# A two-dimensional DFT and a gated layer on one core: the second DFT stage as 64x64 products on four quadrants of the array

## The chip, the cores and the metric

The kernel runs on one core of one Trainium2 chip. The metric is device time in microseconds (us) of one execution, as the median over repeated executions; lower is better. TensorE (PE) does matrix products and writes PSUM; VectorE (DVE), ScalarE (ACT) and GpSimd (POOL) work on SBUF, the first two on PSUM too; SyncE (SP) issues most of the transfers. Each engine runs its own instructions in order and waits on semaphores of the others. In the profile "PE" rows are matmuls and "PEld" rows are the weight loads that go with them.

## The reference

```python
# x: (8, 3008, 256) f32, w_in: (256, 2048), w_out: (2048, 256)
X = np.fft.fft(x, axis=1)
X = np.fft.fft(X, axis=2)
y = X.real.reshape(8 * 3008, 256)
h = y @ w_in
out = (h * np.cos(h)) @ w_out          # (24064, 256)
```

## The kernel before

**How the sums are split.** The DFT over 256 features is folded into the weights once, at the start: `w_in` becomes `WC` (for the real part of the sequence DFT) and `WS` (for its imaginary part). What is left for each of the 8 batches is the DFT over the 3008 positions. 3008 is 47 times 64, and it is done in two stages. The first stage (`first_half` for batch 0, `first_half_later` for the others) takes sums over 47 rows and writes `z` to DRAM, which is read back with its parts in another order (`store_z`, `load_z`). The second stage (`second_half`) takes sums over 64 values with the table `BJ`. It gives, for each of six groups `g` of four columns `jj`, two tiles of 128 features by 256 positions: an "even" part (e = 0, multiplied by `WC`) and an "odd" part (e = 1, multiplied by `WS`), both kept in `pq`. Group 0 uses 225 of the 256 positions (`_width`).

**The table before.** In `z` as loaded, the rows of the even and the odd part are interleaved over the 128 partitions. One matmul for each `jj` contracts all 128 partitions against a 128x128 block of `BJ`, whose columns 0 to 63 give the even part and 64 to 127 the odd part. Half of each block is zero: a row that belongs to the even part has zeros in the odd columns, and the other way round. The four products of a group fill one PSUM bank `pb`, and one ScalarE copy (L540) sorts it into `pq`.

**The main loop.** The gated layer runs in 8 x 6 x 8 = 384 steps: batch, group, and eight pairs of 128-wide slices of the 2048 hidden values (`fp`). A step's work is spread over several turns of the loop at L1068, because it passes through the engines: at turn t the current step `cur` gets its products with `WC` and `WS` (`mm1`, L719) into a PSUM bank `H`; ScalarE doubles it (L730), VectorE subtracts (L735), ScalarE rounds (L750) and takes the sine (L760), VectorE does the rest (L754, L764, L775, L785), and three turns later (`LAG`) `mm2` (L810) multiplies by combinations of `w_out` into accumulators `M`. A turn of 256 positions has two `mm1` products with `WC`, four products of `mm2`, two of `mm1` with `WS`, and three of `mm2`, in this order. Every f32 product appears in the profile as two weight loads and two matmuls.

**PSUM.** Eight banks: `M` four, `H` three, and a single one of tag `fft`, shared in turn by the first stage (`pz`) and the second (`pb`). `H` of the next step is set to 0.25 plus a rank-one term by ScalarE (`seed`, L689) before `mm1` adds to it.

**Where the DFT of the next batch goes.** While batch b-1 goes through the layer, `transform(b)` places the DFT of batch b at turns counted from the start of batch b-1 (offset 0 to 47; 48 and up is the next batch's first turns). First-stage products run at offsets 12, 20, 28 and 36 as a "session" between `mm1(cur, 0)` and `mm2(done, 0)`: 64x64 products on the four quadrants of the array, with two outputs, one in the `fft` bank and one in the `H` bank that the next step will use. ScalarE copies the `H` part out at once (`take_half`), before `seed` overwrites that bank, and the `fft` part at the end of the turn (`take_first`). VectorE folds the input for these sessions (`fold_pair`, L364) at offsets 8 to 11, 16 to 19, and so on, and writes the results of a finished group out by transposes (L912) at offsets 6, 7, 14, 15 and so on. `z` is loaded at offset 38. The six groups of the second stage run at the end of turns 42, 44, 46, 49, 52 and 55 (49, 52 and 55 are turns 1, 4 and 7 of the next batch). Batch 0 has its own places: group 0 in the opening, the others at turns 5, 10, 14, 18 and 22 (`opening`). After each group two small transfers on SP (L549, L550) spread row 0 of the odd part over 128 partitions as `nb`, which `seed` reads.

Of the kernel before, what the change touches and what calls it, by code (L numbers as in the profile page):

```python
# [11 lines left out]
FP = mybir.dt.float32  # L12
# [9 lines left out]
NJ = 24  # L22
# [23 lines left out]
def _consts():  # L46

    s2 = np.arange(N2)  # L50
    j = np.arange(NJ)
    th = 2.0 * np.pi * np.outer(s2, j) / N2
    thm = 2.0 * np.pi * np.outer(46 - s2, j) / N2
    thh = 2.0 * np.pi * np.outer(s2 + 0.5, j) / N2
    z = np.zeros((N2, NJ))
    pad = np.zeros((2 * N2, 16))

    def stack(a, b, c, d):
        m = np.block([[a, b], [c, d]]).reshape(2 * N2, 2, NJ)
        near, far = m[:, :, 0:JA], m[:, :, JA:]  # L60
        return near.reshape(2 * N2, 2 * JA), far.reshape(2 * N2, 2 * (NJ - JA)), pad

    LE = stack(np.cos(th), -np.sin(th), np.cos(thm), -np.sin(thm))
    LO = stack(np.sin(th), np.cos(th), -np.sin(thm), -np.cos(thm))
    LE0 = stack(np.cos(th), z, z, np.cos(thh))
    LO0 = stack(np.sin(th), z, z, np.sin(thh))
    LM, LO, LM0, LO0 = (np.concatenate(m, axis=1) for m in (LE, LO, LE0, LO0))
    LE, LE0 = (np.concatenate(m[::-1], axis=1) for m in (LE, LE0))
    L = np.concatenate([LE, LO, LE0, LO0, -LO, LM, LM0], axis=1)
    rows = np.zeros((128, NL))  # L70
    for side in range(2):
# [12 lines left out]
    i = np.arange(NI)  # L84
    B = np.zeros((128, NJ, 128))
    for jj in range(NJ):
        phi = 2.0 * np.pi * np.outer(i, 47 * k2 + jj) / SEQ
        blk = np.concatenate([np.cos(phi), np.sin(phi)], axis=0)
        blk[0] = 1.0
        blk[NI] = np.where(k2 % 2 == 0, 1.0, -1.0)  # L90
        blk = blk.reshape(2, 2, 16, 64)
        for half in range(2):
            for r in range(2):
                for e in range(2):
                    p = 64 * half + 2 * e + r
                    B[p : p + 61 : 4, jj, 64 * e : 64 * e + 64] = blk[r, half]

    c = np.arange(ND)
    d = np.arange(128)
    ang = 2.0 * np.pi * np.outer(c, d) / ND  # L100
    CS = np.concatenate([np.cos(ang), -np.sin(ang)], axis=1) / TWO_PI
    CS[:, 128] = np.where(c % 2 == 0, 1.0, -1.0) / TWO_PI
    CS = CS[0:128].reshape(128, 2, 64, 2).transpose(0, 1, 3, 2).reshape(128, 256)
    return (
        L.astype(np.float32),
        B.reshape(128, NJ * 128).astype(np.float32),
        CS.astype(np.float32),
    )

# [27 lines left out]
def kernel(  # L137
# [92 lines left out]
    BJ = cpool.tile([128, NJ * 128], FP, tag="BJ", name="BJ")  # L230
    w2 = cpool.tile([128, 16 * ND], FP, tag="w2", name="w2")

    def load_w(q):
# [204 lines left out]
    zss = {}  # L438
    pairs = {}

    def first_half(b, c):

        LE, LO, LE0, LO0, NLO, LM, LM0 = (L[0:XR, 64 * q : 64 * q + 64] for q in range(7))
# [28 lines left out]
                    fv = home(c, e).rearrange("r (i d) -> r i d", d=128)[0:XR]  # L472
                    product(e, i0, i1, e, w[e], fv[:, i0:i1, e:128])
        if c < 4:
            if c // 2 not in pairs:
                pairs[c // 2] = spool.tile([128, 1024], FP, tag="zs", bufs=2, name="zs")
            zs = pairs[c // 2][:, 512 * (c % 2) : 512 * (c % 2) + 512]
        else:
            zs = spool.tile([128, 512], FP, tag="pq", bufs=8, name="zs")
        take_z(zs, pz)  # L480
        zss[b, c] = zs

# [27 lines left out]
            if queue is nc.gpsimd and far:  # L510
                beside(sent, near_z)

    def load_z(b, far, rows=slice(0, 128)):
        if b not in z2s:
            z2s[b] = spool.tile([128, NJ * 128], FP, tag="z2", bufs=1, name="z2")
        cols = slice(128 * JA, None) if far else slice(0, 128 * JA)
        return nc.sync.dma_start(out=z2s[b][rows, cols], in_=zds[b, far][rows])

    ready = {}

    def second_half(b, g):

        T = _width(g)
        z2 = z2s[b]
        pb = psum("pb")
        pq = spool.tile([128, 512], FP, tag="pq", bufs=8, name="pq")
        pv = pq.rearrange("d (e q k) -> d e q k", e=2, k=64)
        bv = pb.rearrange("d (q e k) -> d e q k", q=4, e=2)
        for q in range(4):
            jj = 4 * g + q  # L530
            at = 128 * ((q + 3) % 4 if g == 0 else q)
            nc.tensor.matmul(  # L532
                pb[:, at : at + 128],
                lhsT=z2[:, jj * 128 : jj * 128 + 128],
                rhs=BJ[:, jj * 128 : jj * 128 + 128],
                start=True,
                stop=True,
            )
        if b or g:
            nc.scalar.copy(out=pv, in_=bv)  # L540
        else:
            nc.scalar.copy(out=pv[:, 1], in_=bv[:, 1])
            nc.vector.tensor_copy(out=pv[:, 0], in_=bv[:, 0])
        nb = spool.tile([128, 256], FP, tag="nb", bufs=6, name="nb")
        ready[b, g] = (pq, nb)
        if b == 0 and g < 2:
            return
        nd = dpool.tile([1, 256], FP, tag="nd", bufs=4, name="nd")
        nc.sync.dma_start(out=nd[:, 0:T], in_=pq[0:1, 256 : 256 + T])  # L549
        nc.sync.dma_start(out=nb[:, 0:T], in_=nd[0:1, 0:T].to_broadcast([128, T]))  # L550


    def spread_norm(g, tag):
        T = _width(g)
        pq, nb = ready[0, g]
        pn = psum("pn", tag)
        nc.tensor.matmul(pn[:, 0:T], lhsT=first, rhs=pq[:, 256 : 256 + T], start=True, stop=True)
        return nb[:, 0:T], pn[:, 0:T]

    def keep_norm(out, in_):  # L560
# [7 lines left out]
    def transform(b):  # L568
# [13 lines left out]
                between.setdefault(t0 + o + e + 1, []).append((fold_pair, c, e))  # L582
        for k in range(NCH // 2):
            o = 12 + 8 * k
            sessions[t0 + o] = b, k
            at(o, take_first, b, k)
            at(o + 1, store_z, b, k, 0)
            at(o + 1, store_z, b, k, 1)
# [3 lines left out]
            between.setdefault(t0 + f, []).append((fold_edge, e))  # L592
        at(38, load_z, b, 0)
        at(38, load_z, b, 1)
        for g, o in enumerate((42, 44, 46, 49, 52, 55)):
            at(o, second_half, b, g)

    def split_sum(n):
        nc.vector.tensor_tensor(out=plus[n], in0=wr[n][0], in1=wr[n][1], op=ALU.add)
# [28 lines left out]

    def keep_row(e, n, pw, _):
        if n > 1:  # L630
            nrow[n] = spool.tile([128, 512], FP, tag="pq", bufs=8, name="nrow")
        nc.vector.tensor_copy(out=nrow[n][0:1, :], in_=pw[0:1, :])

    def fold(e, n, tag="M", row=False):
# [66 lines left out]
    def seed_first(s):  # L701
        T, c0 = s.T, 256 * (s.fp % 2)
        s.pq, s.nb = ready[s.b, s.grp]
        for u in range(2):
            nc.tensor.matmul(  # L705
                s.H[:, u * T : u * T + T],
                lhsT=nrow[s.fp // 2][:, c0 + 128 * u : c0 + 128 * u + 128],
                rhs=s.pq[:, 256 : 256 + T],
                start=False,
                stop=True,  # L710
                skip_group_check=True,
            )

    def mm1(s, e):
        T = s.T
        W = WS if e else WC
        for u in range(2):
# [1 line left out]
            nc.tensor.matmul(  # L719
                s.H[:, u * T : u * T + T],  # L720
                lhsT=W[:, 128 * f : 128 * f + 128],
                rhs=s.pq[:, 256 * e : 256 * e + T],
                start=False,
                stop=True,
                skip_group_check=True,
# [235 lines left out]
    for n in range(3):  # L961
# [2 lines left out]
        fill = fold_weights(0, n)  # L964
        keep_fold(*fill)
        if n == 0:
            beside(load_bj(0, 512), fill[3])
        if n < 2:
            split_sum(n + 2)
            split_rest(n + 2)  # L970
        keep_row(*row)
    for s in steps[0:3]:
        fill_first(s)
    load_z(0, 0, slice(0, 112))
    near_z = load_z(0, 0, slice(112, 128))
    for c in order[:4]:
        store_z(0, c, 1)
    for row in range(2):
# [4 lines left out]
    for k, c in enumerate(order[4:]):  # L983
        store_z(0, c, 1)
        if k:
            take_columns((1, 2, 0)[k - 1])
    load_bj(512, 1024)
    second_half(0, 0)
    late = fold_weights(1, 3, units=(0,))
    combine_w2(0, 2, nc.vector)  # L990

    opening = {
        5: ((second_half, 0, 1),),
        6: ((lambda: keep_norm(*spread_norm(1, "fft")),),),
        8: ((load_bj, 1536, NJ * 128),),
        10: ((second_half, 0, 2), (load_ident,)),
        14: ((second_half, 0, 3),),
        18: ((second_half, 0, 4),),
        22: ((second_half, 0, 5),),
    }  # L1000
# [58 lines left out]
    for call in todo.pop(LAG - 1, ()):  # L1059
        call[0](*call[1:])  # L1060
    load_v()
    load_bj(1024, 1536)

    def step(t, last=None):
        s = steps[t] if 0 <= t < n else None
# [2 lines left out]
    for t in range(LAG, n + LAG + 1):  # L1068
# [91 lines left out]
```

## Time and profile before

| | |
|---|---|
| median of 3 runs | 1914.87 us (1914.58 to 1915.2) |
| the profiled execution | 1914.27 us, span 1912.5 us |
| granted TensorE clock, mean | 0.999 of full speed |
| PE matmuls | 9334 records, busy 1899.5 us |
| DVE | 3340 instructions, busy 1782.8 us |
| ACT | 2681 instructions, busy 1490.9 us |
| POOL | busy 414.9 us |
| second-stage matmuls (pb, L532) | 384 records, median 275 ns |
| second-stage copies (pq, L540) | 47, median 585 ns |
| first-stage matmuls of batches 1 to 7 (L396, 64x64 quadrants) | 482 to 642 ns for 384 to 512 columns |

Durations of matmuls overlap, since the next starts while the last one drains; what a matmul costs is read from the distance of two starts. The busy time of an engine is the union of its instructions. The idle time of an engine, and what ended it, is shown beside a group of instructions.

### The profile page before, as it was taken

The numbers are of one execution on the slowest core, as the hardware profiler recorded it, in microseconds if no ns is written. First come the engines' busy times: TensorE is split into PE (matmuls) and PEld (weight loads), VectorE is DVE, ScalarE is ACT, GpSimd is POOL, SyncE is SP. The second block draws the span as 40 slices with busy tenths as digits, with TensorE's granted clock in tenths as the row PEclk, the third lists the DMA queues.
The fourth block names the chain that finished last, engine by engine and source line by source line (L and its number), as shares of the span: only waits on it lengthen the run. The fifth ranks groups of instructions, "written<-read, shape, count | busy, mean of one in ns | idle before, by whom it ended". The sixth has DMA issues, their size and how long they took to land.

```text
span 1912.5 us, 29405 instructions
## 1 busy us (share of the span) xinstructions
PE 1899.5 (99%) x9334; PEld 1688.3 (88%) x9334; DVE 1782.8 (93%) x3340; ACT 1490.9 (78%) x2681; POOL 414.9 (22%) x493
## 2 busy tenths in 40 slices
PE   8999999999999999999999999999999999999998
PEld 5888899888998889988898888988889888898887
DVE  7999989999899998999999999999999999999998
ACT  5777777778777877788777877788777887787775
POOL 5422112221122211222112221122211222111111
PEclk9999999999999999999999999999999999999999
DMA  7321211113111221111311113101231011210001
GB/s 239 81 52 48 79 45 26 27 47 81 38 28 29 49 80 32 31 29 45 88 28 28 28 45 90 31 22 28 54 87 30 19 23 27 59 24 10 13 21 23
DMA packets 157386, 89.15 MB, mean 47 GB/s; under 512 B 106374, under 2 KB 151903, under 8 KB 154891
## 3 DMA queue, kind: packets, MB, share of 16 engines
q1 hardware_dynamic: 153823, 83.48, 17.1%
q0 software_dynamic: 1376, 1.84, 0.4%
q10 hardware_dynamic: 2032, 1.95, 0.3%
q8 instruction: 74, 1.21, 0.3%
q14 instruction: 81, 0.66, 0.1%
HBM read 49.94 MB, written 37.28 MB: 46 GB/s over the span
## 4 chain that ended last, share of the span: by engine, by line
PE 97%; DVE 1%; DMA 0%; issue 0%; ACT 0%; ACTq 0%; SPq 0%; DVEq 0%
PE M L810 59%; PE H L719 34%; PE pb L532 2%; PE pz L396 1%; DMA xp<-in_x_dram 0%; PE pz L453 0%; DVE r L764 0%; PE pw L610 0%; DVE r L754 0%; DVE S L775 0%; PE H L396 0%; DMA z<-zd 0%; DVE h L735 0%; DVE xp L214 0%; PE H L705 0%
## 5 line engine op out<-in xcount | busy, mean ns | idle before, releaser
L810 PE MATMUL M<-S,VX 128*128 128x256 f32 (+1 forms) x2304 | 612.7, 375 | 0.0
L810 PEld LDWEIGHTS M<-S,VX 128*128 128x128 f32 x2304 | 438.6, 190 | 49.1
L750 ACT ACTIVATE r<-H 128x512 f32<-128x512 f32 (+1 forms) x384 | 226.1, 589 | 283.5 <-DVE h L735 280.7
L760 ACT ACTIVATE r<-r 128x1024 f32<-128x1024 f32 (+1 forms) x384 | 395.6, 1030 | 24.6 <-DVE r L754 17.2
L810 PE MATMUL M<-r,w 128*128 128x256 f32 (+1 forms) x1536 | 391.1, 377 | 0.0
L719 PE MATMUL H<-pq,WS 128*128 128x256 f32 (+1 forms) x1536 | 388.1, 375 | 0.9 <-ACT ew L730 0.9
L719 PE MATMUL H<-pq,WC 128*128 128x256 f32 (+1 forms) x1536 | 387.8, 375 | 0.0
L689 ACT ACTIVATE H<-nb,wn 128x256 f32<-128x256 f32 (+1 forms) x762 | 361.2, 474 | 13.3
L735 DVE TENSOR_TENSOR h<-ew,H 128x512 f32<-128x512 f32 (+1 forms) x384 | 259.0, 674 | 94.4 <-PE H L719 86.0
L719 PEld LDWEIGHTS H<-pq,WS 128*128 128x128 f32 x1536 | 292.1, 190 | 34.8 <-ACT ew L730 2.4
L810 PEld LDWEIGHTS M<-r,w 128*128 128x128 f32 x1536 | 298.4, 196 | 26.1
L719 PEld LDWEIGHTS H<-pq,WC 128*128 128x128 f32 x1536 | 288.6, 190 | 29.2
L754 DVE SCALAR_TENSOR_TENSOR r<-r,H 128x512 f32<-128x512 f32 (+1 forms) x384 | 258.7, 674 | 18.0
L730 ACT ACTIVATE ew<-H 128x512 f32<-128x512 f32 (+1 forms) x384 | 225.6, 587 | 51.7 <-PE H L719 45.5
L862 POOL TENSOR_TENSOR cb<-cb,mr 128x256 f32<-128x256 f32 (+3 forms) x190 | 159.3, 849 | 484.8 <-DVE S L785 343.0
L775 DVE TENSOR_TENSOR S<-r 128x512 f32<-128x512 f32 (+1 forms) x384 | 259.7, 676 | 0.1
L754 DVE SCALAR_TENSOR_TENSOR r<-r,h 128x512 f32<-128x512 f32 (+1 forms) x384 | 259.2, 675 | 0.0
L764 DVE SCALAR_TENSOR_TENSOR r<-h,r 128x512 f32<-128x512 f32 (+1 forms) x384 | 258.5, 673 | 0.0
L764 DVE SCALAR_TENSOR_TENSOR r<-H,r 128x512 f32<-128x512 f32 (+1 forms) x384 | 256.3, 667 | 0.4
L750 ACT ACTIVATE r<-h 128x512 f32<-128x512 f32 (+1 forms) x384 | 235.6, 613 | 0.0
L339 POOL TENSOR_TENSOR xs<-xp 113x512 f32<-113x512 f32 x112 | 143.0, 1276 | 403.2 <-DVE S L785 309.9
L810 PE MATMUL M<-S,w 128*128 128x256 f32 (+1 forms) x768 | 226.9, 377 | 1.2 <-DVE S L785 1.1
(106 smaller groups left out, 1531.6 us busy)
## 6 DMA issues: line engine op xcount, KB each, us to landing
out_dram<-ob SPq DMA_DIRECT2D x726, 32.0 KB
xp<-in_x_dram SPq DMA_DIRECT2D x256, 56.0 KB
z<-zd SPq DMA_DIRECT2D x8, 1280.0 KB
zd<-zs SPq DMA_DIRECT2D x120, 80.0 KB
nb<-nd SPq DMA_DIRECT2D x39, 128.0 KB
xp<-in_x_dram SPq DMA_DIRECT2D x52, 48.0 KB
xp<-in_x_dram SPq DMA_DIRECT2D x42, 49.0 KB
w<-in_moe_w_out_dram SPq DMA_DIRECT2D x4, 512.0 KB
```

What stands on the lines that cost most here:

```text
L339: return nc.gpsimd.tensor_tensor(out=rows_of(c, e)[0:XL], in0=xv[:, 0], in1=xv[:, 1], op=ALU.subtract if e else ALU.add,)
L689: nc.scalar.activation(out=s.H[:, u * T : u * T + T], in_=s.nb[:, 0:T], func=AF.Copy, bias=0.25, scale=wn[:, f : f + 1],)
L719: nc.tensor.matmul(s.H[:, u * T : u * T + T], lhsT=W[:, 128 * f : 128 * f + 128], rhs=s.pq[:, 256 * e : 256 * e + T], start=False, stop=Tr ...
L730: nc.scalar.mul(out=s.ew[:, 0 : 2 * s.T], in_=s.H[:, 0 : 2 * s.T], mul=2.0)
L735: return nc.vector.tensor_tensor(out=s.h[:, 0 : 2 * T].rearrange("p (u t) -> p u t", u=2)[:, :, ::-1], in0=s.ew[:, 0 : 2 * T].rearrange("p ...
L750: nc.scalar.activation(out=r, in_=h, func=AF.Copy, bias=BIG, scale=1.0)
L754: nc.vector.scalar_tensor_tensor(out=r, in0=r, scalar=-BIG, in1=h, op0=ALU.add, op1=ALU.subtract)
L760: nc.scalar.activation(out=r, in_=r, func=AF.Sin, bias=0.0, scale=SIN_SCALE)
L764: nc.vector.scalar_tensor_tensor(out=r, in0=h, scalar=-0.25, in1=r, op0=ALU.add, op1=ALU.mult)
L775: return nc.vector.tensor_tensor(out=sv[:, 0:2], in0=gv[:, 2:3].to_broadcast([128, 2, T]), in1=gv[:, 0:4:3], op=ALU.subtract,)
L810: nc.tensor.matmul(acc[key][m // 2][:, 256 * (m % 2) : 256 * (m % 2) + T], lhsT=w, rhs=a, start=first, stop=s.fp == 7, skip_group_check=True,)
L862: return nc.gpsimd.tensor_tensor(out=o, in0=a, in1=b, op=ALU.subtract if less else ALU.add)
```

## The change

The second stage is cut into 64x64 products. The even rows of `z` go to partitions 0 to 63 and the odd rows to 64 to 127 (a transposed read in `load_z`), so `BJ` has one 64x64 block for each part and no zeros, and half its size. Each `jj` takes four products: features 0 to 63 or 64 to 127 (u), times even or odd part (e). The two parts go to different PSUM banks. Two groups are done in one call (`second_pair`), as a session like those of the first stage, with the even part in the `fft` bank and the odd part in the next step's `H` bank. The three calls of a batch stand at offsets 44, 53 and 61. In batch 0, groups 0 and 1 stay single calls, and the others are pairs at turns 13 and 21. `pq`, `nb` and the two small transfers cover two groups at a time.

```diff
-    B = np.zeros((128, NJ, 128))
+    B = np.zeros((128, NJ, 64))
...
-                    p = 64 * half + 2 * e + r
-                    B[p : p + 61 : 4, jj, 64 * e : 64 * e + 64] = blk[r, half]
+                    p = 64 * e + 32 * r + 16 * half
+                    B[p : p + 16, jj] = blk[r, half]
...
-    def load_z(b, far, rows=slice(0, 128)):
+    def load_z(b, far):
...
-        return nc.sync.dma_start(out=z2s[b][rows, cols], in_=zds[b, far][rows])
+        return nc.sync.dma_start(
+            out=z2s[b][:, cols], in_=zds[b, far].rearrange("(x q) c -> q x c", q=4)
+        )
...
-    def second_half(b, g):
-
-        T = _width(g)
+    def second_products(b, groups, homes, clear=(True, True)):
         z2 = z2s[b]
-        pb = psum("pb")
...
-        for q in range(4):
-            jj = 4 * g + q
-            at = 128 * ((q + 3) % 4 if g == 0 else q)
-            nc.tensor.matmul(
-                pb[:, at : at + 128],
-                lhsT=z2[:, jj * 128 : jj * 128 + 128],
-                rhs=BJ[:, jj * 128 : jj * 128 + 128],
-                start=True,
-                stop=True,
-            )
+        for n, g in enumerate(groups):
+            for q in range(4):
+                jj = 4 * g + q
+                at = 256 * n + 64 * ((q + 3) % 4 if g == 0 else q)
+                for u in range(2):
+                    for e in range(2):
+                        first = n == q == 0 and clear[e]
+                        nc.tensor.matmul(
+                            homes[e][64 * u : 64 * u + 64, at : at + 64],
+                            lhsT=z2[64 * e : 64 * e + 64, 128 * jj + 64 * u : 128 * jj + 64 * u + 64],
+                            rhs=BJ[64 * e : 64 * e + 64, 64 * jj : 64 * jj + 64],
+                            start=first,
+                            stop=True,
+                            skip_group_check=not first,
+                        )
...
+    def second_half(g):
+        pb = psum("pb")
+        if g == 0:
+            homes, clear = (pb[:, 0:256], psum("pb", "M")[:, 0:256]), (True, True)
+        else:
+            homes, clear = (pb[:, 0:256], acc[0, 0][3][:, 256:512]), (True, False)
+        second_products(0, (g,), homes, clear)
+        halves = hold(0, g)
+        nc.scalar.copy(out=halves[1], in_=homes[1])
+        (nc.scalar.copy if g else nc.vector.tensor_copy)(out=halves[0], in_=homes[0])
+
+    def second_pair(b, k, after):
+        pb = psum("pb")
+        after.H = psum("H", "H")
+        second_products(b, (2 * k, 2 * k + 1), (pb, after.H))
+        for g in (2 * k, 2 * k + 1):
+            hold(b, g)
+        pqs[b, k] = pb
+
+    def take_pair(b, k, e, src):
+        pq, nb = held[b, k]
+        nc.scalar.copy(out=pq[:, 512 * e : 512 * e + 512], in_=src)
+        if e:
+            nd = dpool.tile([1, 512], FP, tag="nd", bufs=4, name="nd")
+            nc.sync.dma_start(out=nd, in_=pq[0:1, 512:1024])
+            nc.sync.dma_start(out=nb, in_=nd[0:1].to_broadcast([128, 512]))
+
+    def take_plus(b, k):
+        take_pair(b, k, 0, pqs[b, k])
...
-            sessions[t0 + o] = b, k
+            sessions[t0 + o] = first_half_later, take_half, b, k
...
-        for g, o in enumerate((42, 44, 46, 49, 52, 55)):
-            at(o, second_half, b, g)
+        later_pair(t0 + 44, b, 0)
+        later_pair(t0 + 53, b, 1)
+        later_pair(t0 + 61, b, 2)
+
+    def later_pair(t, b, k):
+        sessions[t] = second_pair, take_pair, b, k
+        todo.setdefault(t, []).append((take_plus, b, k))
...
-    load_z(0, 0, slice(0, 112))
-    near_z = load_z(0, 0, slice(112, 128))
+    near_z = load_z(0, 0)
...
-    load_bj(512, 1024)
-    second_half(0, 0)
+    load_bj(256, 512)
+    second_half(0)
...
-        5: ((second_half, 0, 1),),
+        5: ((second_half, 1),),
...
-        8: ((load_bj, 1536, NJ * 128),),
-        10: ((second_half, 0, 2), (load_ident,)),
-        14: ((second_half, 0, 3),),
-        18: ((second_half, 0, 4),),
-        22: ((second_half, 0, 5),),
+        10: ((load_ident,),),
...
+    later_pair(13, 0, 1)
+    later_pair(21, 0, 2)
...
-            first_half_later(*session, step(t + 1))
+            session[0](*session[2:], step(t + 1))
...
-            take_half(*session, 1, step(t + 1).H)
+            session[1](*session[2:], 1, step(t + 1).H)
```

More of the change, by code (lines that the diff above doesn't have):

```diff
@@ L105, in _consts @@
         L.astype(np.float32),
-        B.reshape(128, NJ * 128).astype(np.float32),
+        B.reshape(128, NJ * 64).astype(np.float32),
         CS.astype(np.float32),
@@ L229 @@
     plus = [w[:, 1024:1536] for w in staged[0:2]] + [more[:, 0:512], more[:, 512:1024]]
-    BJ = cpool.tile([128, NJ * 128], FP, tag="BJ", name="BJ")
+    BJ = cpool.tile([128, NJ * 64], FP, tag="BJ", name="BJ")
     w2 = cpool.tile([128, 16 * ND], FP, tag="w2", name="w2")
@@ L439, with half_tile @@
     pairs = {}
+    def half_tile(name, n, tag="pq", bufs=4):
+        at = name, n // 2
+        if at not in pairs:
+            pairs[at] = spool.tile([128, 1024], FP, tag=tag, bufs=bufs, name=name)
+        return pairs[at][:, 512 * (n % 2) : 512 * (n % 2) + 512]
     def first_half(b, c):
@@ L474, in first_half @@
         if c < 4:
-            if c // 2 not in pairs:
-                pairs[c // 2] = spool.tile([128, 1024], FP, tag="zs", bufs=2, name="zs")
-            zs = pairs[c // 2][:, 512 * (c % 2) : 512 * (c % 2) + 512]
+            zs = half_tile("zs", c, "zs", 2)
         else:
-            zs = spool.tile([128, 512], FP, tag="pq", bufs=8, name="zs")
+            zs = half_tile("zs", c)
         take_z(zs, pz)
@@ L516, in load_z @@
         cols = slice(128 * JA, None) if far else slice(0, 128 * JA)
-        return nc.sync.dma_start(out=z2s[b][rows, cols], in_=zds[b, far][rows])
+        return nc.sync.dma_start(
+            out=z2s[b][:, cols], in_=zds[b, far].rearrange("(x q) c -> q x c", q=4)
+        )
     ready = {}
-    def second_half(b, g):
-        T = _width(g)
+    def second_products(b, groups, homes, clear=(True, True)):
         z2 = z2s[b]
-        pb = psum("pb")
-        pq = spool.tile([128, 512], FP, tag="pq", bufs=8, name="pq")
-        pv = pq.rearrange("d (e q k) -> d e q k", e=2, k=64)
-        bv = pb.rearrange("d (q e k) -> d e q k", q=4, e=2)
-        for q in range(4):
-            jj = 4 * g + q
-            at = 128 * ((q + 3) % 4 if g == 0 else q)
-            nc.tensor.matmul(
-                pb[:, at : at + 128],
-                lhsT=z2[:, jj * 128 : jj * 128 + 128],
-                rhs=BJ[:, jj * 128 : jj * 128 + 128],
-                start=True,
-                stop=True,
-            )
-        if b or g:
-            nc.scalar.copy(out=pv, in_=bv)
-        else:
[L542 to L550, printed above, removed]
@@ new lines, in hold @@
+    def hold(b, g):
+        at = b, g // 2
+        if at not in held:
+            held[at] = (
+                spool.tile([128, 1024], FP, tag="pq", bufs=4, name="pq"),
+                spool.tile([128, 512], FP, tag="nb", bufs=3, name="nb"),
+            )
+        pq, nb = held[at]
+        c0 = 256 * (g % 2)
+        halves = pq[:, c0 : c0 + 256], pq[:, 512 + c0 : 768 + c0]
+        ready[b, g] = halves, nb[:, c0 : c0 + 256]
+        return halves
+    held = {}
+    def second_half(g):
+        pb = psum("pb")
+        if g == 0:
+            homes, clear = (pb[:, 0:256], psum("pb", "M")[:, 0:256]), (True, True)
+        else:
+            homes, clear = (pb[:, 0:256], acc[0, 0][3][:, 256:512]), (True, False)
[3 more added lines that the diff above has]
+        (nc.scalar.copy if g else nc.vector.tensor_copy)(out=halves[0], in_=homes[0])
@@ new lines, in second_pair @@
+    def second_pair(b, k, after):
[5 more added lines that the diff above has]
+        pqs[b, k] = pb
+    pqs = {}
+    def take_pair(b, k, e, src):
[5 more added lines that the diff above has]
+            nc.sync.dma_start(out=nb, in_=nd[0:1].to_broadcast([128, 512]))
@@ L556, in spread_norm @@
         pn = psum("pn", tag)
-        nc.tensor.matmul(pn[:, 0:T], lhsT=first, rhs=pq[:, 256 : 256 + T], start=True, stop=True)
+        nc.tensor.matmul(pn[:, 0:T], lhsT=first, rhs=pq[1][:, 0:T], start=True, stop=True)
         return nb[:, 0:T], pn[:, 0:T]
@@ L630, in keep_row @@
         if n > 1:
-            nrow[n] = spool.tile([128, 512], FP, tag="pq", bufs=8, name="nrow")
+            nrow[n] = half_tile("nrow", n)
         nc.vector.tensor_copy(out=nrow[n][0:1, :], in_=pw[0:1, :])
@@ L707, in seed_first @@
                 lhsT=nrow[s.fp // 2][:, c0 + 128 * u : c0 + 128 * u + 128],
-                rhs=s.pq[:, 256 : 256 + T],
+                rhs=s.pq[1][:, 0:T],
                 start=False,
@@ L721, in mm1 @@
                 lhsT=W[:, 128 * f : 128 * f + 128],
-                rhs=s.pq[:, 256 * e : 256 * e + T],
+                rhs=s.pq[e][:, 0:T],
                 start=False,
@@ L966 @@
         if n == 0:
-            beside(load_bj(0, 512), fill[3])
+            beside(load_bj(0, 256), fill[3])
         if n < 2:
@@ L1061 @@
     load_v()
-    load_bj(1024, 1536)
+    load_bj(512, NJ * 64)
     def step(t, last=None):
```

## The prediction

> **What bounds the kernel now.** I read the page's busy shares first, then the chain that ended last.
>
> ```profile
> PE 1899.5 (99%) x9334; PEld 1688.3 (88%) x9334; DVE 1782.8 (93%) x3340; ACT 1490.9 (78%) x2681; POOL 414.9 (22%) x493
> ...
> PE 97%; DVE 1%; DMA 0%; issue 0%; ACT 0%; ACTq 0%; SPq 0%; DVEq 0%
> PE M L810 59%; PE H L719 34%; PE pb L532 2%; PE pz L396 1%; DMA xp<-in_x_dram 0%; PE pz L453 0%; DVE r L764 0%; PE pw L610 0%; DVE r L754 0%; DVE S L775 0%; PE H L396 0%; DMA z<-zd 0%; DVE h L735 0%; DVE xp L214 0%; PE H L705 0%
> ```
>
> PE sets the time from end to end, and the second stage (`pb`, L532) is 2% of it, on that chain. So time taken from it is gained, unless PE then waits. VectorE at 93% is the engine it could wait for.
>
> Next the timeline of PE around one group (columns: start, length, engine, line):
>
> ```profile
> 237.03 1.05 PE L532 MATMUL pb<-BJ,z 128*128 128x128 f32 x8
> 237.92 1.03 PE L719 MATMUL H<-pq,WC 128*128 128x256 f32 x4
> ```
>
> Eight records from 237.03 to 237.92: a group costs 0.89 us, 0.111 for each record. In the second row four records of 256 columns take 0.86 to the next start, 0.215 each, so 0.84 ns a column; 128 columns are 0.107, and each short record pays 0.004 more.
>
> Third, a first-stage session, the only place where all four quadrants work:
>
> ```profile
> 163.66 0.60 PE L719 MATMUL H<-pq,WC 128*128 128x256 f32 x2
> 164.19 0.64 PE L396 MATMUL pz<-xf,V 49*64 49x512 f32 x1
> 164.19 0.64 PE L396 MATMUL H<-xf,V 49*64 49x512 f32 x1
> 164.20 0.64 PE L396 MATMUL pz<-xf,V 49*64 49x512 f32 x1
> 164.21 0.64 PE L396 MATMUL H<-xf,V 49*64 49x512 f32 x1
> 164.66 0.59 PE L396 MATMUL pz<-xf,V 49*64 49x512 f32 x1
> ...
> 165.14 0.20 PE L396 MATMUL pz<-xs,V 49*64 49x4 f32 x1
> ...
> 165.27 1.14 PE L810 MATMUL M<-r,w 128*128 128x256 f32 x4
> ```
>
> Four products start within 0.02 us of each other and run together; their second records follow 0.47 later (427 ns of columns and 0.05 for the first weight load, which nothing hides: 0.64 against 0.59). Entering costs 0.09: the last 256-column record starts at 163.88, is through at 164.09, and the quadrants start at 164.19. Leaving costs 0.12 from 165.14 to 165.27, and 0.11 for the open weight load of the next product (1.14 against 1.03).
>
> **The second stage in quadrants.** A pair of groups is 32 products, 64 records, 16 for each quadrant. A record of 64 columns is 0.054 of columns and, like the short ones above, 0.004 more: 0.058. The weight loads give the same: two single-column records of one quadrant late in a session have their loads 0.06 apart, so a 64-wide load just hides behind 64 columns. Bounds: 0.054, and 0.070 (a 512-column record in a quadrant is followed after 0.443, 16 ns over its columns). I take 0.058, since the record it comes from is the nearest in length. A pair is then 0.09 + 0.05 + 16 x 0.058 + 0.10 + 0.11 = 1.28 us; leaving is taken as 0.10 (0.09 after the fold of the weights at 27.84, 0.12 here). Two groups cost 1.78 now, so 0.50 is saved, for 23 pairs (3 in each of batches 1 to 7, 2 in batch 0): **-11.5 us**. Groups 0 and 1 of batch 0 stay single, 0.82 for 0.89; group 0 lies in the opening where PE waits, and I count 0.3 for it.
>
> **What else moves, at nothing.** ScalarE copies as much as before (two of 0.585 for two groups), but the odd part's copy now comes before the next `seed`; sessions have the same copy there, and the `seed` behind it still ends 2.4 us before its `mm1` (322.58 to 324.95). The SP queue gets 23 row transfers and 23 spreads for 46 each, and the odd part of a pair is there three turns (over 12 us) before `seed` needs it, two turns for the pair at turn 13; in the old timeline a spread is issued 1.1 to 3.6 us after its row. `BJ` is half the bytes. The near `z` load of batch 0 becomes one transfer of 128 rows that waits for the last store, where 112 rows went 0.43 us ahead; PE waited 1.4 us for it. This can cost 0 to 0.5, once; I take 0. The copy from half of an accumulator bank (group 1) can hold `mm2` by at most 0.6, once, in turns where PE waits for VectorE anyway.
>
> **First wait: the `fft` bank.** The last pair of each batch stands at offset 13, one turn after the session at 12, whose even half must leave the bank first:
>
> ```profile
> 324.95 1.03 PE L719 MATMUL H<-pq,WC 128*128 128x256 f32 x4
> ```
> ```profile
> 325.66 0.58 ACT L384 COPY zs<-pz 128x512 f32<-128x512 f32 x1
> ```
>
> PE is through with `mm1` at 325.81 and, with 0.09 to enter, ready for the pair at 325.90. The copy ends at 326.24, and the closest that a matmul follows its input's writer in this trace is 0.05. PE waits 0.39, and behind it in its queue `mm2` and all of the turn. This holds at turns 13, 61, 109, 157, 205, 253, 301 and at 21 (after the session at 20); 349 has no session before it. **+3.1 us** (0 if the copy comes sooner, 4 if the handover takes 0.15).
>
> **Second wait: VectorE at offsets 8 to 11.** There VectorE folds inputs and writes transposes, and a turn of group 0 is short for PE. PE's last product of a turn reads `S`, whose last part VectorE has just written. The two timelines from turn 151 on (offset 7 in batch 3):
>
> ```profile
> 768.15 1.05 PE L532 MATMUL pb<-BJ,z 128*128 128x128 f32 x8
> ...
> 773.06 0.55 PE L810 MATMUL M<-S,w 128*128 128x225 f32 x2
> ...
> 781.84 0.55 PE L810 MATMUL M<-S,w 128*128 128x225 f32 x2
> ...
> 786.54 0.66 PE L810 MATMUL M<-S,w 128*128 128x256 f32 x2
> ```
> ```profile
> 771.85 0.38 DVE L785 TENSOR_TENSOR S<-r,S 128x225 f32<-128x225 f32 x1
> ...
> 781.23 0.38 DVE L785 TENSOR_TENSOR S<-r,S 128x225 f32<-128x225 f32 x1
> ...
> 785.95 0.42 DVE L785 TENSOR_TENSOR S<-r,S 128x256 f32<-128x256 f32 x1
> ```
>
> The margins are 0.83, 0.23 and 0.17 us. From 763 on VectorE has no break but short ones behind its own work (ScalarE's rounding), and 0.11 that it waits for PE before L735 at 772.57. The group at 768.15, which gives it 0.89, goes away; the pair at offset 53 stands too early to help, as VectorE has caught up by 54. So PE comes 0.89 earlier, VectorE 0.11: the margin of 0.17 becomes -0.61, and PE waits 0.61 + 0.05 = 0.66. The session at 12 then gives it all back to VectorE. Six such places (turns 56, 104, 152, 200, 248 and 296): 4.0. In batch 0 the group at turn 10 covers the same stretch, margin 0.49: 0.45. **+4.4 us** (0 to 6.5: none, or a full 0.89 at each). At offsets 42 to 49 the smallest margin left by the same reckoning is 0.3.
>
> **Sum.** -11.5 - 0.3 + 3.1 + 4.4 = -4.3 on the profiled execution's 1914.27 (span 1912.5 and 1.8 around it). The median is 0.6 higher; -4.3 on it gives **1910.6 us**.
>
> **Rivals.**
>
> *The covers hold.* If VectorE's reserve is larger than read and the copy leaves in time, both waits vanish: 1914.9 - 11.8 = 1903; half of them, 1907. For it: VectorE averages 93%. Against: in turns 7 to 10 PE already follows VectorE at 0.05.
>
> *A slow quadrant record.* At 0.070 a pair is 1.47, the saving 7.1 and the sum +0.1: 1915. For it: the 443 ns. Against: two 128-column records of one quadrant follow each other after 0.114.
>
> *Starts are the bound (slower).* The four quadrants run together only if 64 records can be started fast enough. From a spacing of 17 ns on, a pair (64 x 0.017 + 0.35 = 1.44) saves too little to pay for the two waits, and the kernel is slower. The widest spacing of neighbouring starts that the trace could argue for is one quadrant's 0.03 between tiny records (83.71 to 83.74): 64 x 0.03 + 0.35 = 2.27, +0.49 for each pair, 11.3 + 7.2 on top: 1933; at 0.02, 1918. Against: the four starts above, 7 ns apart. For: nowhere does the trace have more than about ten such starts in a row. The Trainium skill, "TensorE: Matmul & The Clock Gate", section "Wait — 56ns, not 53.3ns?", says that starts never come closer than about 25 ns however short the matmul; by that figure a pair is an estimated 1.95 us and the kernel about 1926 us. The 7 ns in the row above disagree, for four in a row.
>
> *The quadrants don't overlap in such a stream* (two at a time), so that the change does not do what it says: 32 x 0.058 + 0.35 = 2.2, near the same 1932; it goes with the third rival.
>
> **Chances.** Forecast with both waits 0.50, its own range 1908 to 1914; covers hold 0.20; slow record 0.08; starts or overlap 0.22. What a measurement here can tell from no change is about 0.2%, 3.8 us, so the line is at 1911.0. Of the forecast's half, 0.30 falls below it and 0.20 above. Faster 0.30 + 0.20 = 0.50; same 0.20 + 0.08 = 0.28; slower 0.22. Range 1904 to 1921: the lower end leaves out only the case of no wait at all, the upper takes in starts up to 0.02 and leaves out most of the rest of that case.
>
> **What would show it.** The distance of two records of one quadrant in a pair (0.058), and from `mm1` to `mm2` around a pair (1.28 more than without). At offset 13, PE idle about 0.4, ended by ScalarE's copy of `pz`. At offsets 8 to 11, PE idle before `M<-S,w` ended by VectorE's L785, about 0.66 a batch; none at 42 to 49. It is wrong if a pair takes over 1.45 us, or PE's waits add up to under 3 or over 11 us.

## The result, and the profile after

| | before | after |
|---|---|---|
| median, runs beside each other | 1914.86 us (1914.58 to 1915.2, 4 runs) | 2004.56 us (2002.4 to 2007.45, 4 runs) |
| the profiled execution | 1914.27 us, span 1912.5 us | 2007.45 us, span 2005.7 us |
| granted TensorE clock, mean | 0.999 | 0.979 |

The change makes the kernel slower by 4.7% (ratio 1.0469, interval 1.0451 to 1.0487). The busy shares and the chain that ended last, in the kernel after:

```profile
PE 1924.3 (96%) x10486; PEld 1684.6 (84%) x10486; DVE 1780.1 (89%) x3340; ACT 1489.3 (74%) x2682; POOL 412.4 (21%) x493
...
PE 79%; DMA 9%; SPq 7%; DVE 2%; ACT 1%; issue 1%; POOL 0%; ACTq 0%; DVEq 0%; POOLq 0%
PE M L854 49%; PE H L763 28%; DMA z<-zd 5%; SPq L966 5%; SPq L182 2%; PE pz L396 1%; DMA xp<-in_x_dram 1%; DMA nd<-pq 1%; DMA nb<-nd 1%; PE pb L536 1%; ACT r L794 1%; DVE r L808 0%; DVE h L779 0%; DVE ob L956 0%; ACT H L733 0%
```

Before, PE was 97% of the chain and no transfer had 1% of it. Now it is 79%, and the load of `z` (L521), the stores on SP (L966), the loads of `x` (L182) and the spread of row 0 (`nd`, `nb`) stand in it. The waits name the same two transfers (columns: who waited for what, us in total, times, longest):

```profile
ACT H L733 <- DMA nb<-nd: 40.8, 6, 7.7
PE pb L536 <- DMA z<-zd: 39.6, 9, 9.8
...
PE H L763 <- ACT H L733: 27.3, 6, 5.5
...
PEld pb L536 <- ACT zs L384: 5.7, 8, 0.7
```

Next the timeline of SP around the load for batch 2, after (start, length until the last of the group is issued, line):

```profile
488.01 1.19 SPq L521 DMA_DIRECT2D z<-zd  x2
489.29 24.38 SPq L966 DMA_DIRECT2D out_dram<-ob  x8
513.77 15.65 SPq L182 DMA_DIRECT2D xp<-in_x_dram  x28
529.53 0.24 SPq L586 DMA_DIRECT2D nd<-pq  x1
533.50 0.36 SPq L587 DMA_DIRECT2D nb<-nd  x1
```

Eight stores take 24.38 us to issue. In the kernel before, eight stores behind the same load took this:

```profile
457.46 1.35 SPq L517 DMA_DIRECT2D z<-zd  x2
458.91 7.69 SPq L922 DMA_DIRECT2D out_dram<-ob  x8
```

The windows show how the load itself runs (columns: window, length, busy time of five engines with instructions, granted clock, mean busy share of the 16 DMA engines, GB/s). After, and then before, from the load's issue on:

```profile
492.00:497.00 5.00, 5.00 (x25) 4.45 (x24) 4.90 (x9) 4.04 (x8) 0.00 (x0) 1.00 0.26 74
497.00:502.00 5.00, 5.00 (x25) 4.44 (x24) 4.68 (x9) 4.72 (x9) 0.00 (x0) 1.00 0.25 74
...
507.00:512.00 5.00, 0.85 (x34) 0.56 (x32) 2.69 (x6) 0.61 (x2) 1.26 (x1) 0.83 0.21 64
512.00:517.00 5.00, 4.84 (x41) 4.01 (x42) 0.00 (x0) 2.52 (x4) 0.00 (x0) 0.50 0.23 57
```
```profile
457.00:462.00 5.00, 5.00 (x25) 4.43 (x24) 5.00 (x10) 3.75 (x7) 0.00 (x0) 1.00 0.74 209
462.00:467.00 5.00, 5.00 (x25) 4.46 (x24) 4.87 (x10) 4.04 (x8) 0.00 (x0) 1.00 0.51 165
...
464.00:465.00 1.00, 1.00 (x6) 0.88 (x5) 1.00 (x3) 1.00 (x2) 0.00 (x0) 1.00 0.31 88
```

Before, 0.74 of the DMA engines work in the mean of the first window, and by 464, some 6 us behind the issue, the rate has fallen to the 88 GB/s of what else was under way: the load is through. After, the share stays between 0.21 and 0.26, about a quarter of the 16 engines, at 64 to 85 GB/s, until the far part lands at 512. The packets in the two traces fit this: in the mean 12.7 are under way at a time while the far part runs before, and 4.0 after, though its 128 packets take about as much time together (62 us before, 69 after). At 507 to 512 PE has 0.85 us of work in 5: it waits for `z`. In the window after that its clock is at 0.50.

The length of a turn is read as the distance between the starts of the first `mm1` product (`H<-pq,WC`) of two steps. Compared turn by turn with the kernel before, the difference adds up as follows (batches 1 to 7 by offset; 93.6 at the last step, to the rounding of the rows):

| where | difference, us | what the rows there show |
|---|---|---|
| opening, up to turn 4 | +4.5 | group 0 later: its `z` lands later |
| batch 0, turns 5 to 8 | +10.5 | group 1 waits for the far part of `z` |
| offset 44, 7 turns, beyond the pair | +38.2 | the pair waits for the far part of `z` |
| offsets 47 and 0, 6 each | +28.2 and +15.0 | `seed` waits for `nb`, `mm1` for `seed`, clock low behind it |
| everything that the prediction reckoned with | -2.9 | pairs, `fft` bank, VectorE |

The last row is the prediction's own sum of -4.3, short by 1.4. The rest, 96.5 us, stands where transfers are waited for; the experiments below show that it comes from the load of `z`, which the prediction took at nothing.

### The profile page after: what moved, and what is told of

Read it like the earlier page. It is cut to its first block, busy times and chain, and to the rows that moved or that the text cites. A ratio compares the mean times of both kernels' runs of the same rounds, so it can differ in the third digit from the quotient of the medians.

```text
span 2005.7 us, 31628 instructions
## 1 busy us (share of the span) xinstructions
PE 1924.3 (96%) x10486; PEld 1684.6 (84%) x10486; DVE 1780.1 (89%) x3340; ACT 1489.3 (74%) x2682; POOL 412.4 (21%) x493
## 4 chain that ended last, share of the span: by engine, by line
PE 79%; DMA 9%; SPq 7%; DVE 2%; ACT 1%; issue 1%; POOL 0%; ACTq 0%; DVEq 0%; POOLq 0%
PE M L854 49%; PE H L763 28%; DMA z<-zd 5%; SPq L966 5%; SPq L182 2%; PE pz L396 1%; DMA xp<-in_x_dram 1%; DMA nd<-pq 1%; DMA nb<-nd 1%; PE pb L536 1%; ACT r L794 1%; DVE r L808 0%; DVE h L779 0%; DVE ob L956 0%; ACT H L733 0%
## 5 line engine op out<-in xcount | busy, mean ns | idle before, releaser
L763 PE MATMUL H<-pq,WC 128*128 128x256 f32 (+1 forms) x1536 | 393.9, 379 | 27.3 <-ACT H L733 27.3
L854 PE MATMUL M<-r,w 128*128 128x256 f32 (+1 forms) x1536 | 404.2, 386 | 0.0
L733 ACT ACTIVATE H<-nb,wn 128x256 f32<-128x256 f32 (+1 forms) x762 | 361.9, 475 | 54.9 <-DMA nb<-nd 40.8
L763 PEld LDWEIGHTS H<-pq,WC 128*128 128x128 f32 x1536 | 294.3, 192 | 61.1 <-ACT H L733 29.6
L854 PEld LDWEIGHTS M<-r,w 128*128 128x128 f32 x1536 | 302.5, 200 | 29.8
L854 PE MATMUL M<-r,VX 128*128 128x256 f32 (+1 forms) x768 | 229.7, 381 | 0.0
```

The lines of the kernel that those rows point to most:

```text
L733: nc.scalar.activation(out=s.H[:, u * T : u * T + T], in_=s.nb[:, 0:T], func=AF.Copy, bias=0.25, scale=wn[:, f : f + 1],)
L763: nc.tensor.matmul(s.H[:, u * T : u * T + T], lhsT=W[:, 128 * f : 128 * f + 128], rhs=s.pq[e][:, 0:T], start=False, stop=True, skip_group_ ...
L854: nc.tensor.matmul(acc[key][m // 2][:, 256 * (m % 2) : 256 * (m % 2) + T], lhsT=w, rhs=a, start=first, stop=s.fp == 7, skip_group_check=True,)
```

## The experiments

The theory: the transposed read makes the load's outer dimension 4 (`q`), only four of the 16 DMA engines carry it, and it lands too late; transfers that share those engines are late with it. The rivals: the pairs themselves or the moved places cost more than reckoned, or it is the order of the rows in DRAM, not the number of engines.

### The load as four transfers

```diff
-        return nc.sync.dma_start(
-            out=z2s[b][:, cols], in_=zds[b, far].rearrange("(x q) c -> q x c", q=4)
-        )
+        rows = zds[b, far].rearrange("(x q) c -> q x c", q=4)
+        for q in range(4):
+            sent = nc.sync.dma_start(out=z2s[b][32 * q : 32 * q + 32, cols], in_=rows[q])
+        return sent
```

> The changed kernel, with each load of z as four transfers of 32 rows (one for each quarter of the partitions) in place of one transfer whose outer dimension is 4. The rows read, their order and the table are the same. Theory A (a transfer with an outer dimension of 4 is worked on by 4 of the 16 DMA engines, so that z and all that stands behind it on the SP queue come late): the packets of the load overlap 12 to 14 deep as before the change, not 4; far z lands within 10 us; no wait for z at offset 44 and none for nb at 47; what is left are the pair (+1.29 a turn), 0.38 at offset 13 and 0.7 at offsets 8 to 11, so 11.3 - 3.0 - 4.7 = 3.6 us under the old time: 1909 to 1913 us. Theory B (rows read from DRAM in steps of four are slow, however they are split): 4 deep or as slow as now, 1980 to 2005 us. Theory C (the pairs themselves keep the other transfers back): the load is fast, the waits for nb stay, 1930 to 1980 us.

1914.95 us (ratio 1.0004, interval 0.9995 to 1.0014): the 4.7% are gone, with the same rows in the same order, but it is 2 us over the 1909 to 1913 of theory A. Two windows behind the load's issue at 462.80, for this kernel:

```profile
463.00:467.00 4.00, 4.00 (x20) 3.57 (x19) 4.00 (x9) 2.77 (x5) 0.00 (x0) 1.00 0.64 173
467.00:471.00 4.00, 4.00 (x21) 3.54 (x20) 3.93 (x8) 3.56 (x6) 0.00 (x0) 1.00 1.05 220
```

All 16 engines work again. By turns, offset 44 is +0.41 (a pair for a group) and 47 and 0 are as before. From turn 10 on the main loop is 2.8 us shorter than before, as the last row of the table has it. Batch 0 takes this back: turns 5, 6 and 8 are +3.3, +1.0 and +1.1, for a wait that is left there (PE, timeline):

```profile
51.57 0.32 PE L537 MATMUL pb<-BJ,z 64*64 64x64 f32 x2
54.65 0.34 PE L537 MATMUL M<-BJ,z 64*64 64x64 f32 x1 [2.76 <-DMA z<-zd]
...
55.70 1.87 PE L764 MATMUL H<-pq,WC 128*128 128x225 f32 x4
```

The far part of `z` lands at 54.5, some 3 us behind the call's first records; the four `mm1` records after it take 1.87 instead of 0.92. In the kernel before, group 1 waited for nothing there: it started at 51.80, and the last packet of its far part had ended at 48.1. Here that packet ends at 53.1, though the load was issued 2 us sooner (from 39.15 on, against 41.15); why the packets of the four transfers take 13 us there from first to last, where those of one took 6, was not tried.

### The load alone, in the kernel before

Before, with the transposed load in one transfer and the table's rows permuted to suit; the zeros, the single groups and their places stay.

```diff
-                    p = 64 * half + 2 * e + r
-                    B[p : p + 61 : 4, jj, 64 * e : 64 * e + 64] = blk[r, half]
+                    p = 64 * e + 32 * r + 16 * half
+                    B[p : p + 16, jj, 64 * e : 64 * e + 64] = blk[r, half]
...
-        return nc.sync.dma_start(out=z2s[b][rows, cols], in_=zds[b, far][rows])
+        return nc.sync.dma_start(
+            out=z2s[b][:, cols], in_=zds[b, far].rearrange("(x q) c -> q x c", q=4)
+        )
...
-    load_z(0, 0, slice(0, 112))
-    near_z = load_z(0, 0, slice(112, 128))
+    near_z = load_z(0, 0)
```

> The kernel before, with the new order of z's rows alone: the transposed load in one transfer, and the 128x128 table (with its zeros) with its rows in that order. Its products, their places and their transfers are the old ones. Theory A: the load overlaps 4 deep and takes 20 us or more; PE hardly waits for z itself, since the far part is first needed at the end of turn 44, but the row transfers of group 0 stand behind it on SP, so seed waits for nb at offset 47: 1935 to 1985 us. Theory C (it is the pairs): 1912 to 1918 us.

One run: 1963.92 us. Two windows behind the load's issue at 479.84, for this kernel:

```profile
480.00:485.00 5.00, 5.00 (x24) 4.42 (x24) 4.94 (x10) 3.74 (x7) 0.00 (x0) 1.00 0.25 77
485.00:490.00 5.00, 5.00 (x25) 4.45 (x24) 4.93 (x10) 3.81 (x8) 0.00 (x0) 1.00 0.26 95
```

Without any pair the load costs some 50 us, at the same share of the engines. `nb` is late behind it here too (ScalarE waits 33.5 us for it, 40.8 after). It costs less than in the changed kernel, and by turns the place is offset 44, which adds 0.2 us here in place of 38.2. In the trace of batch 2, group 1 stands at the end of that turn (504.0), 5 us after the last packet of the far part (498.8); the pair of the changed kernel stands ahead of the rest of the turn (507.15), and its far part lands at 512.1.

### Two transfers with an outer dimension of 2

```diff
-        for q in range(4):
-            sent = nc.sync.dma_start(out=z2s[b][32 * q : 32 * q + 32, cols], in_=rows[q])
+        for q in (0, 2):
+            sent = nc.sync.dma_start(
+                out=z2s[b][32 * q : 32 * q + 64, cols], in_=rows[q : q + 2]
+            )
```

> The changed kernel with each load of z as two transfers with an outer dimension of 2. Theory A1 (outer element i goes to engine i, from the same first engine each time): both transfers work on the same 2 engines, z lands some 40 us after its issue, overlap 2 deep: 2100 us or more. Theory A2 (2 engines each, but other ones): overlap 4 deep, about as the changed kernel, 1990 to 2010 us. Theory B: about as the changed kernel too, with any overlap.

One run: 2124.82 us. The windows behind the load's issue at 516.5, for this kernel:

```profile
528.00:533.00 5.00, 5.00 (x25) 4.42 (x25) 4.71 (x10) 4.71 (x10) 0.00 (x0) 1.00 0.12 33
533.00:538.00 5.00, 3.38 (x45) 2.66 (x43) 4.70 (x10) 2.97 (x5) 1.42 (x2) 1.00 0.13 38
538.00:543.00 5.00, 0.00 (x0) 0.00 (x0) 0.21 (x1) 0.00 (x0) 1.26 (x1) 0.61 0.14 50
```

A share of 0.12 to 0.14 is about two engines of 16 (0.125), half of the 0.25 with an outer dimension of 4, though the load is two transfers: the second goes to the same two engines, as theory A1 has it, or it runs only behind the first; the share doesn't tell these two apart. So what counts is the outer dimension of a transfer; neither the number of transfers nor the order of the rows explains this. The Trainium skill, "DMA: Bandwidth & Descriptors", states this in "Rules for kernel authors": an outermost dimension below 16 confines a transfer to at most that many engines. By that rule alone the load here gets at most 4 of 16; the measured shares of 0.25 and 0.12 agree, and so do the shares of 0.64 and 1.05 with 32 rows outermost.

### The load issued by ScalarE

The changed kernel, with `z` of batches 1 to 7 issued from ScalarE's queue, still with an outer dimension of 4.

```diff
-        return nc.sync.dma_start(
+        queue = nc.scalar if b else nc.sync
+        return queue.dma_start(
```

> The changed kernel with the loads of z of batches 1 to 7 issued by ScalarE instead of SP, nothing else moved (still one transfer with an outer dimension of 4). Theory (SP's queue is the second cost: the stores, the loads of x and the spread nb stand behind the slow load in SP's own queue): nb is in time, the waits at offset 47 and 0 (together some 7 a batch) go, those for z at offset 44 stay: 1950 to 1965, and ScalarE's waits for nb fall from 41 to under 10. Rival (the four DMA engines that carry the load hold up every transfer that shares them, whichever queue issued it): nb is as late as before, 1990 to 2010. A third way: ScalarE itself is held at the issue, and seed and rounding come late for it: above 2010.

1998.6 us (ratio 1.0429, interval 1.0408 to 1.0451): what the rival gave. The timeline of SP for this kernel:

```profile
482.32 30.65 SPq L967 DMA_DIRECT2D out_dram<-ob  x16
513.07 15.69 SPq L182 DMA_DIRECT2D xp<-in_x_dram  x28
528.86 0.24 SPq L587 DMA_DIRECT2D nd<-pq  x1
532.51 0.36 SPq L588 DMA_DIRECT2D nb<-nd  x1
```

ScalarE issues the two parts at 481.86 and 482.58, 6 us sooner than SP did behind its stores, and with that nearly all of the wait at offset 44 is gone (+1.2 beyond the pairs in place of +38.2), which I had expected to stay. The load is sooner, not faster: the last packet of its far part ends at 506.75, 24 us behind its issue. But SP is held just as long (16 stores take 30.65 us) though no slow load is in its queue, and `nb` is issued by 532.9, in the changed kernel by 533.9. ScalarE's waits for `nb` rise from 40.8 to 67.9 us, and offset 47 takes +55.3 in place of +28.2. So my theory of SP's order fell, and the rival fits. The packets show the hold itself; a store's are of 256 bytes. The rows are for eight stores in the kernel before with no load under way (452.6 to 457.4), for the changed kernel during the load (490 to 506), and for this one during the load (488 to 499):

```profile
DMA packets 793, 0.21 MB, mean 44 GB/s; under 512 B 792, under 2 KB 792, under 8 KB 792
DMA packets 216, 1.25 MB, mean 78 GB/s; under 512 B 4, under 2 KB 4, under 8 KB 116
DMA packets 148, 0.78 MB, mean 71 GB/s; under 512 B 74, under 2 KB 74, under 8 KB 74
```

Stores behind the load in one queue stand still, and stores in another queue go at some 7 packets a us in place of some 165. The other lesson is that the wait for `z` was not the bound alone: 27 of the 37 us that go at offset 44 come back at 47, as waits for `nb`.

### The pairs at other places

Four transfers as above, and the pairs where the two predicted waits should not arise: away from the turn behind a session, and at the turn where VectorE is behind.

```diff
-        later_pair(t0 + 53, b, 1)
-        later_pair(t0 + 61, b, 2)
+        later_pair(t0 + 56, b, 1)
+        later_pair(t0 + 62, b, 2)
...
-    later_pair(13, 0, 1)
-    later_pair(21, 0, 2)
+    later_pair(10, 0, 1)
+    later_pair(22, 0, 2)
```

> split4 with the pairs of a batch at offsets 44, 56 and 62 in place of 44, 53 and 61, and in batch 0 at turns 10 and 22 in place of 13 and 21. Theory (the two waits of the prediction): one turn after a session no pair has to wait for the copy of pz, which gives back 0.38 x 8 = 3.0 us; a pair in turn 56 gives VectorE 1.29 us just where it is late, which gives back 0.70 in six batches and 0.5 in batch 0, 4.7 us: 7 to 8 us under split4, 1902 to 1906 us. Rival (VectorE's lateness only moves, to turns 54 and 55 or to turn 57 on): 2.5 to 4 us under split4, 1906 to 1909 us.

1909.37 us (ratio 0.9975, interval 0.9966 to 0.9985), 5.6 under the same kernel with the pairs where the change put them: more than the rival's 2.5 to 4, less than the theory's 7 to 8. By turns, the wait for the `fft` bank is gone at all eight places: 13 is 1.68 shorter (the pair's 1.30 and the 0.38) and 14 is 1.30 longer. The waits at 57 and 58 are gone too, but turn 56 is 1.78 longer than before where a pair explains 1.30. The timeline of PE in batch 4 shows why:

```profile
999.68 1.03 PE L764 MATMUL H<-pq,WC 128*128 128x256 f32 x4
1000.64 0.33 PE L537 MATMUL pb<-BJ,z 64*64 64x64 f32 x2
1001.13 0.24 PE L537 MATMUL H<-BJ,z 64*64 64x64 f32 x1 [0.17 <-DVE r L809]
```

The odd half needs the `H` bank that the next step will use, and VectorE's L809 has not read it yet. The wait for VectorE comes back in another form, at 0.48 for 0.72.

### The second pair one turn sooner

```diff
-        later_pair(t0 + 56, b, 1)
+        later_pair(t0 + 55, b, 1)
```

> The kernel with the pairs at offsets 44, 56 and 62, with the second pair at 55 instead of 56. In the run with 56, PE stood idle some 0.3 before the pair for the H bank that VectorE (L809) had not yet read, and the turn was 0.48 longer than the pair alone explains. Theory (VectorE is behind only from the turn after 55 on, so the pair must stand just ahead of it and not in it): no such wait at 55 and none at 56 to 58, 6 x 0.48 = 2.9 less, about 1906.5 (1905.5 to 1908). Rival 1 (VectorE is already behind at 55): the bank wait comes along, 1909 to 1910. Rival 2 (at 55 VectorE has nothing to catch up on, so that the pair there does not help): the waits of 0.17 and 0.30 at 57 and 58 come back, 1909 to 1911.

1910.46 us (ratio 0.9976, interval 0.9966 to 0.9986), no gain. Against the kernel with 56, turn 55 is 1.47 longer (0.17 over the pair), turn 58 has 0.28 of its wait back and turn 59 is 0.07 longer: 0.52 in all for 0.48. Both rivals held in part. What VectorE lacks there is paid at each of the three places that were tried; 53 pays 0.72, and 0.07 at turn 59.

### Group 1 of batch 0 a turn later, and both

```diff
-        5: ((second_half, 1),),
-        6: ((lambda: keep_norm(*spread_norm(1, "fft")),),),
+        6: ((second_half, 1), (lambda: keep_norm(*spread_norm(1, "fft")),)),
```

> The kernel with the pairs at offsets 44, 56 and 62, with the single call of group 1 in batch 0 at turn 6 instead of 5 (ahead of the norm of that turn). Theory (the call came 2.8 before its part of z had landed at 54.5, and PE ran at a low clock after that idle): by turn 6, 4.2 later, z is there; the wait of 2.8 and the slow products behind it go, 4 to 5.5 less, 1904 to 1905.5. Rival 1: only the wait goes, 1906 to 1907. Rival 2: seed of the first step of group 1 then waits for nb, which is issued a turn later behind the loads of x on SP, 2 to 5 back: 1907 to 1910, with ScalarE waiting for nb around turn 8.

1908.10 us (ratio 0.9970, interval 0.9957 to 0.9982). By turns it is 2.8 shorter than the kernel with moved pairs: 0.4 in the opening, 5.2 at turns 5 and 6, and turns 7 and 8 take 2.9 back. The wait for `z` is gone; in its place VectorE waits for the product that spreads the norm, which now comes a turn closer to its use, and PE for VectorE. From the waits between 50 and 75 us:

```profile
DVE nb L601 <- PE pn L597: 2.4, 1, 2.4
PE M L855 <- DVE S L830: 2.3, 2, 1.6
```

So rival 2 had the size and the place, but not the mechanism (no transfer of `nb` is awaited there).

The same edit together with the second pair at 55:

> Both moves together (second pair at 55, group 1 of batch 0 at turn 6). They lie in different batches, so the gains should add: 1901 to 1903 if both theories hold, 1904 to 1907 if one of them does.

1909.65 us (ratio 0.9974, interval 0.9964 to 0.9984): the two do not add, as the move to 55 had nothing to add. Between the last four kernels the intervals overlap; the traces place the one with group 1 later first, the times alone don't. Each of them beats the kernel before by 0.24 to 0.30%.

## Why the prediction was wrong

The step that failed is "What else moves, at nothing". It counts row transfers and spreads and the bytes of `BJ`, looks at the near load of batch 0 alone ("This can cost 0 to 0.5, once; I take 0"), and puts the transposed load of every batch at nothing without pricing how it runs. The far part went from some 7 us, issue to last packet (ended at 464.7), to 23.5 (issued at 488.6, landed at 512.1 in batch 2); 81 us of the result came with it at offsets 44, 47 and 0, and 15 more in the opening and batch 0. The same paragraph gave the odd part of a pair "three turns" of time and a spread issued "1.1 to 3.6 us after its row": in the kernel after, the row itself is issued only at 529.5, behind the stores and the loads of `x`, and the spread at 533.5. The trace of before had one half of the price: 1536 KB kept about three quarters of the DMA engines busy for 7 us (0.74 in the first 5), so a form that keeps a quarter of them busy takes about 20 us, an estimate, and the far part had six turns, some 28 us, between its place at 38 and the call at 44, of which SP's stores ahead of it take 5. The other half, that the transposed form keeps only a quarter busy, is in no row that the prediction shows; the windows after have it at 0.25.

- *A pair:* predicted 1.28, measured 1.29 to 1.30. Right, also in its parts. One pair in the kernel after (start, length, of the first and the last records and the product behind):

```profile
807.74 0.27 PE L536 MATMUL pb<-BJ,z 64*64 64x64 f32 x1
807.74 0.27 PE L536 MATMUL H<-BJ,z 64*64 64x64 f32 x1
807.75 0.27 PE L536 MATMUL pb<-BJ,z 64*64 64x64 f32 x1
807.75 0.27 PE L536 MATMUL H<-BJ,z 64*64 64x64 f32 x1
807.84 0.22 PE L536 MATMUL pb<-BJ,z 64*64 64x64 f32 x1
...
808.67 0.22 PE L536 MATMUL pb<-BJ,z 64*64 64x64 f32 x1
808.68 0.22 PE L536 MATMUL H<-BJ,z 64*64 64x64 f32 x1
808.83 1.04 PE L854 MATMUL M<-r,w 128*128 128x225 f32 x4
```

  Sixty-four records start within 0.94 us, 0.015 apart; in one quadrant they follow at 0.058 behind a first step of 0.10. The 23 pairs save 23 x 0.48 = 11.0 (predicted 11.5, and 0.3 for the opening, where the late `z` costs 4.5 instead).
- *The `fft` bank:* predicted 0.39 at eight places, measured 0.38 at eight (the row `PEld pb L536 <- ACT zs L384`, and [0.32 <-ACT zs L384] beside the first record at 846.99). Right.
- *VectorE at 8 to 11:* predicted 0.66 a batch and 0.45 in batch 0, measured 0.72 and 0.62. The mechanism was right; 4.4 became 4.9. Where I put it, all at the turn of the smallest margin, was too simple: it is paid in parts at 56, 57 and 58 (0.25, 0.17, 0.30). Turn 59 is 0.07 longer too, which the profile doesn't put down to VectorE.
- *The rivals:* none had a DMA in it. "Starts are the bound", which carried the chance of slower, did not happen: 0.015 a start is under the 0.017 from which it would have decided (worked out again, the sum turns at 0.0175). The figure of about 25 ns from the Trainium skill, "TensorE: Matmul & The Clock Gate", section "Wait — 56ns, not 53.3ns?", does not hold for four quadrants in turn: here 64 starts in a row come at 15 ns.
- With the load in four transfers the sum is -2.8 from turn 10 on, for -4.3. Batch 0 was mis-sized there as well: +5.4 at turns 5 to 8, because group 1 had 3.7 us to spare behind the far part of `z` and the far part ends 4.9 later.

## What to carry to other kernels

A rearranged access pattern with the same bytes is a new transfer: look at its outermost dimension first, then ask how long the old transfer took, on what share of the DMA engines, and how many turns it has until its reader. If a read must be transposed, cut it so that each transfer has many rows outermost; eight transfers of 32 rows take 3.67 us of SP's time a batch where two took 1.19, and the kernel was 90 us faster. And price a wait together with what would be late next: with nearly all of the wait for `z` gone, `nb` took its place, and a pair moved away from VectorE's late data met VectorE at the bank it writes to.

## What the runs showed of the hardware

- The share of busy DMA engines follows the outer dimension: 0.21 to 0.26 for 4 and 0.12 to 0.14 for 2, up to 0.79 before (462 to 464, the end of the load) and 1.05 (by the profile's reckoning) with 32 rows outermost.
- A long load holds up other transfers while it runs. In the kernel before the stores stand too, but the load is over in 7 us. With the load in another engine's queue 16 stores still took 30.65 us. On a quarter of the engines, one issue of a store on SP stood for 16.31 us behind it (chain that ended last, after):

```profile
490.82 16.31 SPq L966
```

- After PE stood still for 4.3 us the clock was 0.50 in the next window (512 to 517, after). In the kernel with four transfers, after a stand of 2.8 us, it was 0.50 from 55.7 to 57.5, and there four 225-column `mm1` records took 1.87 us instead of 0.92. So a wait costs more than its length: turns 47 and 0 are 43.2 us longer in all, of which PE waited 27.3 for `seed`. How much of the other 15.9 is the clock was not measured by itself.
